# Another stored order of issue for all engines of an attention and channel-mix kernel

## The chip, the cores and the metric

The kernel runs on one core of a Trainium2 chip. Times are device microseconds of that core: the median of several executions, and one execution that the hardware profiler recorded, with its span from the first to the last instruction. The names of the engines in the profile are PE (TensorE, matmuls), PEld (its weight loads), DVE (VectorE), ACT (ScalarE), POOL (GpSimd) and SP (SyncE, which issues the transfers).

## The reference

Attention with queries averaged in pairs, over 8 batches and 8 heads, 1152 keys of 64 elements; then a channel mix over the attention's output, which is regarded as 8 sequences of 576 rows and 512 columns. All in float32.

```python
q_pool = q.reshape(B, H, S // 2, 2, D).mean(axis=3)            # 8, 8, 576, 64
scores = 1.0 / np.sqrt(D) * np.matmul(q_pool, k.transpose(0, 1, 3, 2))
attn = np.exp(scores - np.max(scores, axis=-1, keepdims=True))
attn = attn / (np.sum(attn, axis=-1, keepdims=True) + 1e-09)
x = np.matmul(attn, v).transpose(0, 2, 1, 3).reshape(8, 576, 512)
x_prev = x shifted by one row, zeros first
xk = mu_k * x + (1.0 - mu_k) * x_prev;  xr = mu_r * x + (1.0 - mu_r) * x_prev
kk = np.maximum(xk @ w_k, 0.0)                                 # 512 to 1024
out = 1.0 / (1.0 + np.exp(-(xr @ w_r))) * (kk * kk @ w_v)      # 1024 to 512
```

## The kernel before

**Numbers.** Operands are split into a high and a low 16-bit part, and products are summed from two or three matmuls on these parts in float32.

**Attention.** There are 64 heads (`n`), and each has 6 blocks (`j`) of 96 pooled queries, 384 blocks in all. A block goes through a chain that visits three engines. TensorE computes 9 score matmuls of 96 columns (L555, in two steps of 4 and 5) into one of three PSUM buffers `s`. VectorE takes the maximum over a block's keys (L562). TensorE transposes it (L565), VectorE reduces it again (L569), and TensorE spreads its negative (L571). ScalarE writes it into a row of the low part of the queries (L575). TensorE adds the second half of the scores with that row (L581, again 4 and 5 matmuls), and ScalarE takes the exponential into `pf` (L587). GpSimd makes its low part (L590). Five windows of queries per head are then multiplied with the values into the one PSUM buffer `a` (L624, L627, L629 and L634), which ScalarE and VectorE empty and normalise (L650 to L686).

**Preparation of heads.** Queries and keys are loaded, split on ScalarE, VectorE and GpSimd (L442, L445, L449, L488, L493), and transposed by a transfer; values are split on ScalarE and VectorE (L522, L525). For the very first head TensorE transposes instead, and ScalarE and VectorE copy the results out of PSUM: the keys for the first scores (L501, L502) and for the second (L513, L514).

**Channel mix.** Once a batch's 8 heads are done, tiles of 256 rows are mixed with their previous rows (L800, L803, L809, L811) and go through three products: 18 tiles with 96 matmuls of 256 columns and 2 x 36 of 512 columns (L831), with ScalarE, VectorE and GpSimd steps on their results (L858 to L895). A batch's mix runs beside the next batches' attention. The weights are loaded and split in the first microseconds.

**The order.** All steps are first collected in a list `ops` with their buffers read and written, from which the dependences follow. Then `Issue.run` reads, for each of the five queues (transfers, VectorE, ScalarE, TensorE, GpSimd), the order of its steps from the stored string `TURNS`: each byte says which of the steps that are left, counted in program order, is issued next.

```python
turns = iter(zlib.decompress(base64.b85decode(turns)))
for e in ENGINES:
    left = [n for n in range(len(ops)) if eng[n] == e]
    while left:
        k = 0
        while (step := next(turns)) == 255:
            k += 255
        order.append(left.pop(k + step))
```

Each engine keeps to that order. A step that waits for another engine therefore holds everything behind it in its own list. `Issue.gaps` puts spare matmuls on zeros (L937) into pauses of TensorE that the planned order has in the first 150 us.

Of the kernel before, what the change touches and what calls it, by code (L numbers as in the profile page):

```python
# [37 lines left out]
LO, VLO = 2.0 ** -28, 2.0 ** -12  # L38
# [17 lines left out]
    ")8(Mc@#X9S3bP4&!b>uFHJz?ZE666xlIdg;CCKD*`CKlY)iRlECYFxHVmU3Ft<SQc`umbZG#<(2Q(2~nmPmz@;Z!&rjz^<uEtN^7QyLOMD;A5#tf*"
    "yKv2;A0N~J7$S%SqZvO+2=sL^Q5AB~hm)UXoqhP{^83tuc5gB5Xy!w3cZmKC%l%v`P-R9DwHtE>E#E|=3;=B%!CR-n8Q4Q9PrS5aG8Q&ZVkU6ILTY"
    "Eg|uWql@*s;$$jYpM~8Y0-jKUDI3^kH@uglpzwTt_ejdE5o63;=43cf;<YrP>|bz-=B$Cfq>=LbTyk)(}@HSb4K0ep0L}Qi^UO*X8jJNOot;Ji#wv"
    "G$(~ydrz3(eN5OD9Vu+fR&afFWgQdZaxNZbYBNWo(!GuST8%D&?bv{ENkPiejk5AW<?4ugcRjqMiqt&1_sC9L9nqH%7npRt<*3_siY8|JpzFw`b18"
    "O+F>55csc}*r$mCGq8)YOitNu{c)Qt6D6LRqO2jn?N1P)bXoghH^&Ei0V0j6hD$L=40*&J$BLm&?Ttt1(L(9_5p}yhKW*x;hexLJ#xFX9NlQu(vxD"  # L60
    "O6o+Z88N~}FKKG&R-p9+az+ojgO=45t96)>3nEc7?9hWjL$}X_JeE%W8P$e<stXl<zdzuI&nrpliutDmn*2^f_tcK5Rco~6foi?d(96pUdKpwjD=1"
    "2-qU0;{s3_M^h$rItd>)C!gz=fu81k!lMk$XL;?YvI1^JRlG*XCUk|~6ZAW{L&Tp*g!BYuu?JchARwP^QLbp~1kku#iLH3%hO80W$p3eO4kg+k`aV"
    "9;bA{JxN>TYTtoy6(|ACG6-m0iR#?$J1z8y6H5$#zh=7gYebc0#RDDkRC*%7KoBz;gF{B#3Cz3PSd1l)*Op89J$FH**UUP51H+zVW`90YGYGt+lp3"
    "Ab?cg{HmF$CQqkPp(p*ugl-KK+RjZd5s!&&7x3;di`TTO0SCkY`Q(ID9QsT&?tPG{dX3C9hx=b&@>_nnm>nTH7x+I^ET|jDTskEBRBbQJSPAx?+k<"
    "%?JozA4KRM1Mq;ud%0IORA{>9n3orN^h`@u<utnaoB0vUDkUQYYIz0VI?8q=ysdRg<oGJS(ka%9$Y836`)UOmM|4lNQbsv?e0ZV48KNzN)5nWKB(t"
    "S#7dhuU=GBUFI<Br9mpyD=RB?b|_h!ETocEU6qxn%WK?2tg1pSYb{Tdl||JBkp<CQG+G)dRV55UkuXX~(`*o#bXS@)lgJtIY&J6@6pZA}GeWvFRGA"
    "E`BztrDh%XfN@wo%~RImT0w9n^FcoRfX93HPH;YqY2z9p7PSzeDCPsY78LC#3n?V<gSXzY=LU2-}|Wn;ckZjhx`fChh-9@K-DE6{2h>xQ2{Z1^x;Z"
    "#Er<QCHVe*V0_8yFKiAGu1?Is6V-(9$Kwl)05M3*$U2_T3y|k&8oS&+PX}QmdsRUGWudQSz3h!2~Eis%A&CtB9U-9S`sc%bI4|cvM<SGE>H38NC&O"
    "9lH{5ByiVcD&C7-|p-|qRh#MKJERagVoAqj5k0<5v(B8%{G97ih-HEt%aUkmTBy~06h*ig8YgNuzDC9D!W?`xsA?(l%sS<$#J9%<Ic2oBTlOa83#f"
    "Dpv7Q<*VOj_4seLeYcR+CwMhS^YGVYKM;YvgP~lNPzMO0AUWDl4lht*TVB<H~DO=^C{PN~NNptWXw@#`B1l71+Uio~yEOIDZ1B=5pbz-IWmX31s6L"  # L70
    "y(6ucSXMqK=QHE;bKrf5W}_*eH|g_fh$K?(q}#0~WG_7)kLnIO3GqmnLTtq_CK`>pso@B@EN39n5^=bkx)s#}rXyrpx?WNmkW|*)Ze2GVWH>v{3^G"
    "@vyCaiE4+U-yADhV@8#rB1VZiRK#uF-~lg@?VR27593Yaiv{FpJ5mC=(Xp*Ue|u{gSjF&I5<v^u(2oK#dgMuOz;RFvZMsiTWiitVG6w$6@@*7gzYt"
    "!-_s7!I_x4{IIQ*4o-)3`2`Dbr_nOo7#pc!^hPRYpHK(ZZ@0h(9obX)KdU!s%z?N>g(#->uQafDpWO9S5=`Bqbka4&|Zz2ipr|W$}+XQQZFknDOG4"
    "U3kpheC0QB=oR&i>lOczasXR`elj+stz1oSf6K5$i5t%_d8kruQK64soO%3;ir=5T))22+F7@HECKu2LhSQ$5AlpkZqc6OpT)(QZgqPt_%$WiPd(B"
    "f)#sKb=H=3#Y;(PTCnRrN-rUf-mmv7t~8rK$#H)n%21((;lD-Jmw1)YNh%sl3Cmhm?LN!j)mNv@8}=bI~A4pNK}Ra7<MqO4vu>`hq@1@zVJWhy89J"
    "3SL(LnHIlaf!AAWn(i<?(Q?b>aVoBP1{^xAJ^@a<ZUzlws-c^T^!&PDj-O>Z#wuf#(WARZYsFEc$0)_3g5szV7}Y+iUC!32UF{vCFrpJ3%E;mEozv"
    "(-wY0S~w+=U3TG&0Kv7-@6Ydsnim9B7k6>*^$d6YZL+-5ePZAfS9(isCV5{jWkTa-w%62{6<Fj*6>j>PHLL?R1-kUvE4#zJ6J5S3PiHxLX3$VyMZ-"
    "{A3i;Pt?b5oJM-*Xed=d<q&p9>wD}4CiT%0_Z%K$=;F8OPsTu^r0y()?6bzg*~O03`fsceGJ__4U;=M%#INl(ca!6dpUi?{1M$9ZD?)NThTgf7$>i"
    "}xpSC~=7~zvaJ8{zOpDr7r`Fc1suz<d*Mcx>EJt~v0&qA>r?^NBN8U6!Woi0GNdj1nDZ@EUG}8z!3tLM<OG435d3$tmgpNfZKwDNHEJgxWND2C9TE"
    "P%nf-OGFXDNPv4F}M}nd2I6ug~veM?F=hNoUvt$6A-`eBJp&kM5BUAW3MN>(-fu?6}MHEm)}Q^XFd(%$qwG+R1SAs`GKu>>r?a&YXVZq*=4(%z<&@"  # L80
    "i9MK!l|3^~IHBjH$c!2KtP`e9)2HimF;zpiI%P7H3($pei@ff!=pF+UyU1|USlrp!KHW51TU$GfHU%xihRsq5RZMGWXlbZ#s<(zUz(Q?9^$FE=b+q"
    "vmypvEp9yJXWJ=GOewN*8=Bd&^4Pf1yMnX1sSq&J3iZdf6wrwnsFJ#1a4E1gJgNh*lvE=;P)L^!S>6pIDRY0DxjBf(%OG@HQ}Z5oj>eQFphx=-r%`"
    "KFvXdGcg}u4}?-cNZqOUE?OWCyX6Go<(Ekj~O|#cnU_Lv(wN!_0EpA5k|*?&JJUQ&W^P<w>GOSEiJ0j)Q$G$`sOC9advav%wS_<ZDVbHJ!&yA)J3C"
    "GQwuuIHU63!R8<wK3KbRODhdtd%8VIRK6hb6c|k2#)v~Ngzd4noRmqsCRwG$fnoTFtDFu2`Q7htV?1FeG6p36MVYebyBpi-K)>TBU^NEU3AUL1m3V"
    "$l@w`QLaB(eQ7faz}cw5ijkPQ|))(*8KR-QLN-<cTJF(KY+biCyM|31h~LqsKAYDC)+9*~N}=#Zet26&-3vYwHNDt*s3huHv*4TAGG851Tu87?g%4"
    "rD+^HThCyj0rjXut+%R~HfeOVw+f6Ks=ZTCSyoo=Eui3(^8`m4lk?eJwz*_{%49rbW=CcdiF8{sm2t#VDIkiNmVgpt$P=YVH-%P*8diliT9KedMXL"
    "<bOr1@F(?PP}^ZSzsoE{DI1Uw$!bOomby1TK|>6|<X=#qFFw~F(3vOZ3qF!oGSA3J8zm{Frg>BUhBjcbRd%xZ5Np%&ZQ(b1-y(yp{Y8Q#<+d5b2cv"
    "Av#xQQxR2v&J+wHPklL)|0(N>IAo^q8jC>C@Xgtob8Oo3rePmvCf!Ml+f_%nM9ghOl9&3qdv<XWunO_EgCz-hYya5un(b7l<^yh9cn_5j+Z|WgjGN"
    "V9R@E$dyhBg^(q7{12Vu=eDIpODMeOB+*C_OnMN!r<rHx)R1Nsy_RBC^#-P;DNL)sv!6<D<2s8#X=N`Ap0G#I(J6Z+Q<6C>5noF}HV{10&_XApKsp"
    "fW5!_$oP{S<42HO(pSWq28o@HkJglJnqV>;uyTpA|kM5bzp?+YLtDmNSuXI(<=JE*J6nIDbr;Xqszc!9tez17lOUhR1?k!OO4`bhJY5WYTT9`6%Hu"  # L90
    "QlXNPq04Csk&os080?wX%V0s4SuC~WL(Al(Bkl}1oqQ-(N~c}Kk<)fPbOcIDcmY+<$K#j}@wivENVDi;5eLA-o4MVAcpw%Cq|*qOAe4*S&6buX>?a"
    "7@_u*sN17-n9B<$v7j}y*7j6H_zQ_`Q1-C-+oH0<Z}B$JSH<dG&l9CmT=oN##QM9@sT1Ia)lpGagm{xlgrpMBr*und&h1-qLZU^?7khVzo-Y(5gP@"
    "4$P@apousuka2HmGB841m{VFm^E4SuYbw)cSEHnvn>4*`1ac`zW7@Bh5u`zLMUH-C7k$99uE$FGdL&<2EP;fcY}ivyjB>W{_E54J{2xze9Eg23kRF"
    "~`fJ%V(^ns|b@k{`fuln+A|%jw>yNQ--$$Q(v=4s<K6(Rt_kMg}@B4%J^mTlISMlC^z@bCHo+C&0?D;$J0-k^S`H%3&eZX^gbMIa}`^K|x?S1?0H{"
    "X2r-FMmG8y|l7^wW3?*#8QTUV38B6HfrY!HbXMu|ML`=U#mDQI`Mj8v}cvdyZ`}?cwswE3Z8G;DdPTf!{x{>wyRGyPrS#G@g0petG)tyYI$hczoBc"
    "NAJY1@d$o}Up~s>C!W~3bLTI1;=h1faPz}A<0jn5;(NK=dg~qAw{O2~`}XfyboniK06zzA*vW&7?*KO6fUCKC%Qj%cWtVN+fbISL*Ysa4%P!%vdGp"
    "qx3oq*1y7lU-`!-?Kg{!b~<w~IciY=F8J+SnG3opQuCD^ofE$gk{v}y6;AFjP*?P8hEU%VJtv<|D+uSef`3sx;yux1Tb%l1|P+*`M9*)m}E?Aa_ib"
    "LLF+oOX848Z2BmV+OCA4mwNAm!CdwUN@CsGUebD-sj}5u2V4wC)rO`EcW#FoLnsS7H3iUP91p)FPg^kDO@H_pEGAz*RTmw=v}vTwM>}O(t;CC;E9H"
    "Dm@%WC7ju6seb@?&ESIUPtGu<Nl{+XDS_&B1-igN6M!HF$y&b{pTGPdJI^But##B{GCNx$;REUcDii$*{I#HDnnS>}6r3nbyzNjc?j)@pVf;?xyBT"
    "^#EEcZwq3112Qu#jvJapnL#vW7=;#3L+^Od<@oNHV)17`E7~@UXs%SKG|_{BwEwb2|yQTodL;$Px(0*I$44osDjxGLsyKNd@6JeE6Hgb`p;7z984W"  # L100
    "`TX-k$BrGc)0eW^Az>apbVz8jE#M2ABZ^QyJMhJU1IM9s=<lQe$%PL-IK1!BP}yt1EBGsS-hTVQ+wV&_lSqHS`>($a{OwP`|8To&|0{ocWf$;!{O;"
    "ez{Z9i-uMG@5KR{UjJN;*uh<%uV-ua8Wciz8KBK<BF-gW%st#{sc=e^r^4uSl?Bu#E1&~Lu+MqCD53jFZ4Yj7)Y<(2sH=FK;39=hm9xc>U9F1@tBp"
    "BVlTaK(>t4Q@RDN7v)Lt>^vFuCWbUuI%gUyS#4`*Vx?OkBhKzBWXfX$nzHfMEKc@H!a?{c=0*dLOlOqAxI9M>pS&SoV%VF$FgOs&go@3t9M!NxyyU"
    "cCSP#&*-Mt3c;boNL(iI?9-M~7%L)30tWK<VcQ5T;!rfC>te7-u5hhNYGf^Ucd{56D;6ws{-e{aUdvWo!VsU1%hrkDYg*nqZdOPM!o!ZmUfe|Cnjc"
    "!Q+8}74bH#LoIveUSxCZ3dO1SXHJnOLOHRLv`j7+*QAvUAFm%E}QVDmyDHY1PX|4d*hdh2A3TlS3m%wjd`{u`Y+sY_=*}Sx4^yO&B79<Uk@($wj0k"
# [872 lines left out]
```

## Time and profile before

| what | value |
|---|---|
| median of 3 executions | 1097.0 us (1094.77 to 1098.14) |
| profiled execution, its own time | 1095.32 us |
| its span | 1093.5 us |
| granted clock of TensorE, mean | 1.00 |
| busy: PE, DVE, ACT, POOL | 1071.0, 886.8, 867.7, 808.6 us |
| moved by transfers | 134.77 MB |

The span is what the rows are measured in; the profiled execution's own time is 1.8 us longer than it. Busy times are sums of drawn durations: matmuls are drawn longer than they keep the engine, since they overlap.

### The profile page before, as it was taken

The numbers are of one execution on the slowest core, as the hardware profiler recorded it, in microseconds if no ns is written. First come the engines' busy times: TensorE is split into PE (matmuls) and PEld (weight loads), VectorE is DVE, ScalarE is ACT, GpSimd is POOL, SyncE is SP. The second block draws the span as 40 slices with busy tenths as digits, with TensorE's granted clock in tenths as the row PEclk, the third lists the DMA queues.
The fourth block names the chain that finished last, engine by engine and source line by source line (L and its number), as shares of the span: only waits on it lengthen the run. The fifth ranks groups of instructions, "written<-read, shape, count | busy, mean of one in ns | idle before, by whom it ended". The sixth has DMA issues, their size and how long they took to land. (4 is left out here: it accounts for less than half of the span.)

```text
span 1093.5 us, 40142 instructions
## 1 busy us (share of the span) xinstructions
PE 1071.0 (98%) x16475; PEld 880.5 (81%) x16475; DVE 886.8 (81%) x1869; ACT 867.7 (79%) x1918; POOL 808.6 (74%) x940
## 2 busy tenths in 40 slices
...
GB/s 215 200 237 203 187 124 147 139 125 147 127 117 154 123 115 143 129 133 123 101 115 126 127 121 116 129 115 142 104 140 134 94 142 84 96 49 34 10 30 31
DMA packets 257387, 134.77 MB, mean 123 GB/s; under 512 B 192753, under 2 KB 229617, under 8 KB 257201
## 3 DMA queue, kind: packets, MB, share of 16 engines
...
q8 instruction: 129, 2.11, 0.8%
...
## 5 line engine op out<-in xcount | busy, mean ns | idle before, releaser
L562 DVE TENSOR_REDUCE mx<-s 128x96 f16<-128x864 f32 x384 | 400.4, 1053 | 69.4 <-PE s L555 40.1
L590 POOL TENSOR_SCALAR pl<-pf 128x864 f16<-128x864 uint16 (+1 forms) x384 | 334.1, 870 | 109.3 <-ACT pf L587 65.8
L587 ACT ACTIVATE pf<-s 128x864 int32<-128x864 f32 x384 | 336.5, 888 | 62.2 <-PE s L581 45.5
L555 PE MATMUL s<-qT,ks 128*128 128x96 f16 x3456 | 237.4, 206 | 2.9 <-ACT pf L587 1.4
L624 PE MATMUL a<-vt,pf 128*128 128x129 f16 x2520 | 234.9, 220 | 0.9 <-DVE den L667 0.6
L581 PE MATMUL s<-qT,ks 128*128 128x96 f16 x3456 | 230.3, 206 | 0.9 <-ACT qT L575 0.4
L555 PEld LDWEIGHTS <-ks 128*128 128x128 f16 x3456 | 191.3, 98 | 25.4 <-issue 3.5
L581 PEld LDWEIGHTS <-ks 128*128 128x128 f16 x3456 | 188.8, 98 | 25.1 <-issue 1.8
L624 PEld LDWEIGHTS <-pf 128*128 128x128 f16 x2520 | 169.0, 98 | 23.5 <-issue 1.6
L569 DVE TENSOR_REDUCE mb<-s 128x1 f16<-128x128 f32 x384 | 108.7, 287 | 42.7 <-PE s L565 37.0
L575 ACT ACTIVATE qT<-s 1x96 f16<-1x96 f32 x384 | 90.1, 236 | 67.0 <-PE s L571 56.9
L634 PE MATMUL a<-vb,pl 128*128 128x65 f16 x2304 | 136.1, 193 | 0.0
L831 PE MATMUL f<-xhk,wk_lo 128*128 128x256 f16 x496 | 135.2, 273 | 0.0
L831 PE MATMUL f<-xhk,wk_hi 128*128 128x256 f16 x496 | 135.2, 273 | 0.0
L831 PE MATMUL f<-xlk,wk_hi 128*128 128x256 f16 x496 | 135.2, 273 | 0.0
L634 PEld LDWEIGHTS <-pl 128*128 128x128 f16 x2304 | 111.1, 98 | 15.4
L831 PEld LDWEIGHTS <-wk_hi 128*128 128x128 f16 x1152 | 104.0, 98 | 13.3
L493 POOL TENSOR_TENSOR kn<-kr,kn 128x320 f16<-128x320 f32 (+1 forms) x126 | 98.9, 789 | 15.5 <-ACT kn L488 9.3
L862 POOL TENSOR_TENSOR gl<-g 128x512 f16<-128x512 f32 x72 | 76.6, 1068 | 43.9 <-ACT g L860 40.6
L831 PE MATMUL f<-wv_hi,g 128*128 128x512 f16 x240 | 90.9, 379 | 0.7 <-ACT ex L879 0.7
L831 PE MATMUL f<-wv_hi,gl 128*128 128x512 f16 x240 | 91.0, 379 | 0.0
L831 PE MATMUL f<-wv_lo,g 128*128 128x512 f16 x240 | 90.9, 379 | 0.0
(128 smaller groups left out, 2166.1 us busy)
## 6 DMA issues: line engine op xcount, KB each, us to landing
...
```

The costliest lines, as they stand in the source:

```text
L493: lambda cs=cs, en=nc.vector if ve else nc.gpsimd: en.tensor_tensor(kn[i][:, cs, D:P], kr[i][:, cs], kn[i][:, cs, 0:D], op=ALU.subtract),
L555: nc.tensor.matmul(cols(c, c + 1), ks1[hp][:, c, :], qhi, start=(c == c0), stop=False, skip_group_check=True)
L562: op("DVE", 0.974, lambda: nc.vector.tensor_reduce(mxz[:, P - QN:P], grid(0, NC).rearrange("p c q -> p q c"), axis=AX.X, op=ALU.max), r=[( ...
L569: op("DVE", 0.199, lambda: nc.vector.tensor_reduce(mbz, s[:, 0:P], axis=AX.X, op=ALU.max), r=[("s", z)], w=[("mb", z)], key=t + O_MAX)
L575: op("ACT", 0.15, lambda: nc.scalar.activation(qlo[0:1], s[0:1, 0:QN], AF.Prelu, scale=1.0 - EPS, alpha=(1.0 + EPS) / (1.0 - EPS)), r=[("s ...
L581: nc.tensor.matmul(cols(c, c + 1), ks2[hp][:, c, :], qlo, start=False, stop=True, skip_group_check=True)
L587: op("ACT", NC * QN / 1200 + 0.051, lambda: nc.scalar.activation(pf[:, :, HALF + rows.start:HALF + rows.stop], grid(0, NC), AF.Exp, bias=S ...
L590: op("POOL", 0.93 if buf == ("pside",) else NC * (r1 - r0) / 1200 + 0.273, lambda: nc.gpsimd.tensor_scalar(to, half(pf, U16, 0)[:, :, HALF ...
L624: nc.tensor.matmul(a_b[:, a0:a0 + D + VN], half(pf, F16, 1)[:, c, his], vt[jv][:, c, 0:D + VN], start=(first and c == 0), stop=(side and c ...
L634: nc.tensor.matmul(av, pl[:, c, rows], vb[jv][:, c, 0:VN], start=False, stop=(c == NC - 1), skip_group_check=True)
L831: nc.tensor.matmul(ps, terms[i][0], terms[i][1], start=(first and i == 0), stop=(i == last), skip_group_check=True)
L862: op("POOL", 2 * n * 0.0018 + 0.14, lambda f2=f2: nc.gpsimd.tensor_tensor(gl[:, f2, 0:n], g32[:, f2, 0:n], gh[:, f2, 0:n], op=ALU.subtract ...
```

## The change

The string `TURNS` is replaced, and nothing else. Both strings hold the same number of steps for each queue, and the steps, their operands and their buffers are the same; the dependences still hold. The core of the diff, 100 lines of encoded text in place of 101:

```diff
 TURNS = (
-    "c-mch37i$hx&7(&?)UcH_j_mN&b|-K3^Q<9hh+d65XOa7R6v#iS6~n#XfP@+L2=E)7<Y~OOyWdMG!dU-qT+MI1eYYJXbggmL=m^t|5Ohq@At3z^;T"
...
+    "c-m!pcYqbu{r#Ex=JlCZ=Jm4W?Y@26cU@Svuq-S^dRYO*0wO4~Dp*kw6-#1AG>K8rBo^$(NP<aBf=Y}=qTj?4j7Ag1M58En4eI>PoyGXa@7|raGjq"
...
 )
```

Decoded, the two lists compare as follows. A neighbour pair is two steps that directly follow each other in both lists.

| queue | steps | at the same place | neighbour pairs kept | mean shift, places | largest shift |
|---|---|---|---|---|---|
| transfers | 496 | 120 | 89 | 2.1 | 16 |
| DVE | 1851 | 301 | 401 | 4.1 | 58 |
| ACT | 1917 | 249 | 387 | 4.5 | 47 |
| PE | 5948 | 1071 | 1475 | 3.0 | 30 |
| POOL | 932 | 121 | 104 | 3.7 | 33 |

The heads of two lists, as an example (`c0` and `c5` are the first five and the last four of the nine key chunks):

```
ACT before: L445 qn, L488 kn c0, L488 kn c5, L467 qT, L488 head 1 c5, L513 keys for the second product, L501 keys for the first, L488 head 1 c0, L404, L467, L522 c5, L522 c0, L445, L575 block 2, ...
ACT after:  L445 qn, L488 kn c5, L488 kn c0, L467 qT, L404, L488 head 1 c0, L501 keys for the first, L488 head 1 c5, L513 keys for the second product, L467, L445, L522 c0, L522 head 1 c0, L522 c5, L488 head 2 c0, L575 block 2, ...
DVE before: L442, L493 c0, L493 c5, L449, L514, L502, L442, L562 block 2, L562 block 0, L569 block 2, ...
DVE after:  L442, L493 c5, L493 c0, L449, L502, L442, L514, L562 block 0, L562 block 2, L449, L569 block 2, ...
```

## Rows read from the trace of the kernel before

**Rows 1.** The page: span, and busy time, share and instructions of engines.

```profile
span 1093.5 us, 40142 instructions
...
PE 1071.0 (98%) x16475; PEld 880.5 (81%) x16475; DVE 886.8 (81%) x1869; ACT 867.7 (79%) x1918; POOL 808.6 (74%) x940
```

**Rows 2.** Windows: length, busy PE, PEld, DVE, ACT, POOL, then PEclk, DMA share, GB/s.

```profile
0.00:60.00 60.00, 51.51 (x1086) 46.72 (x1087) 49.31 (x110) 48.25 (x101) 38.79 (x53) 1.00 0.96 215
60.00:130.00 70.00, 66.69 (x1428) 60.87 (x1425) 67.00 (x130) 67.41 (x149) 61.43 (x70) 1.00 0.78 198
130.00:200.00 70.00, 67.69 (x1014) 55.11 (x1012) 63.59 (x121) 61.04 (x135) 57.39 (x64) 1.00 0.60 146
200.00:600.00 400.00, 397.58 (x6186) 329.98 (x6185) 347.80 (x744) 328.71 (x738) 314.59 (x367) 1.00 0.59 128
600.00:1000.00 400.00, 398.34 (x6194) 332.83 (x6193) 333.62 (x717) 317.45 (x709) 304.76 (x351) 1.00 0.50 110
```

**Rows 3.** Timeline of PE: start, drawn us, line, tile, shape, count, idle before it.

```profile
0.99 3.62 PE L937 MATMUL a<-zero 128*128 128x128 f16 x33 [0.99 <-DVE kn L372]
...
304.42 0.44 PE L634 MATMUL a<-vb,pl 128*128 128x65 f16 x9
304.69 0.33 PE L624 MATMUL a<-vt,pf 128*128 128x129 f16 x3
304.86 0.38 PE L555 MATMUL s<-qT,ks 128*128 128x96 f16 x5
...
306.87 0.55 PE L581 MATMUL s<-qT,ks 128*128 128x96 f16 x9
307.25 0.27 PE L831 MATMUL f<-xhk,wk_hi 128*128 128x256 f16 x1
...
308.33 0.27 PE L831 MATMUL f<-xhk,wk_hi 128*128 128x256 f16 x1
...
309.20 0.33 PE L581 MATMUL s<-qT,ks 128*128 128x96 f16 x4
...
1089.13 0.38 PE L831 MATMUL s<-wv_hi,g 128*128 128x512 f16 x1
...
1089.56 0.38 PE L831 MATMUL s<-wv_hi,gl 128*128 128x512 f16 x1
```

**Rows 4.** DVE groups by line: whole run, whole run, to 130 us, from 130.

```profile
L562 DVE TENSOR_REDUCE mx<-s 128x96 f16<-128x864 f32 x384 | 400.4, 1053 | 69.4 <-PE s L555 40.1
...
L569 DVE TENSOR_REDUCE mb<-s 128x1 f16<-128x128 f32 x384 | 108.7, 287 | 42.7 <-PE s L565 37.0
...
L525 DVE SCALAR_TENSOR_TENSOR vt<-vr,vt 128x256 f16<-128x256 f32 (+1 forms) x18 | 8.5, 481 | 0.0
...
L525 DVE SCALAR_TENSOR_TENSOR vt<-vr,vt 128x320 f16<-128x320 f32 (+1 forms) x110 | 66.0, 603 | 0.3 <-ACT vt L522 0.2
```

**Rows 5.** Timeline of DVE, POOL and PE around 343 us.

```profile
340.94 0.32 DVE L803 SCALAR_TENSOR_TENSOR xk<-xt,mu_k,tmp 128x128 f32<-128x128 f32 x1
...
342.60 1.65 POOL L696 TENSOR_TENSOR st<-xb,st 128x640 f16<-128x640 f32 x1 [2.29 <-ACT st L694]
...
342.91 1.49 DVE L803 SCALAR_TENSOR_TENSOR xk<-xt,mu_k,tmp 128x128 f32<-128x128 f32 x1
...
344.32 1.04 DVE L562 TENSOR_REDUCE mx<-s 128x96 f16<-128x864 f32 x1
...
345.43 0.23 PE L565 MATMUL s<-identb,mx 128*128 128x128 f16 x1 [1.39 <-DVE mx L562]
```

**Rows 6.** Timeline of ACT and PE at the start of the run.

```profile
7.24 0.69 ACT L513 COPY ks<-s 64x640 f16<-64x640 f16 x1 [0.37 <-DVE ks L514]
...
7.95 0.69 ACT L501 COPY ks<-s 128x640 f16<-128x640 f16 x1
...
8.70 0.94 PE L555 MATMUL s<-qT,ks 128*128 128x96 f16 x18 [0.90 <-ACT ks L501]
...
12.22 0.44 ACT L575 ACTIVATE qT<-s 1x96 f16<-1x96 f32 x2 [1.36 <-PE s L937]
```

More of the change, by code (lines that the diff above doesn't have):

```diff
@@ L56 @@
[L56 to L105, printed above, removed]
@@ new lines @@
+    "$*m`!Msmo?&C%&~@AGC?km}Fbr=vW*Aw+U}GchgE#L9W<7@K(KstU&PLG#Pgu>UP!vP+XvMH6s%eU<1bm2bnu9sRFlCSI_r^?kINQ3IY}NE~>>dxN"
+    "U4_oO;2^nFB1zCCus382az2A}38`GFI+aOD$sF?ed?BCD<dkeSm$fstZReF7Q{~$e$yg#*C>EH~N-Ua8C$gz%IvS0}qcJ7LZqg|wnUHNWZpY1-X`1"
+    "nL#!jV7wgO_YcqkeQSs@eQxHyVc#e&fQtW?w=G5vmjkY{awI1-KctPsLsGaU9ZHK6Qms4p9JbwR_ZF^qDZQ7WMY&3cpGSgO=DG_;n=+1hNj(tuQb8"
+    "p%pJ)ley`^{7*9rA8??B&rgLTGZHx)HPHh<yb5dtt~{VBUM%rr2=ZKh=oEplrznc6*gsAN$2ELDh(vcKASfdHByO0HsQ@1exH$+Ql3<jQyq`!Q8O~"
+    "eV|Zd7Pb89RiRd0Z9tS*8)#|ZSQw`_10#UIOwl%dJgA!3tZJA0q98iL)B6Emwu2}2jNtUO%xrHNA8)a24D@tRNQjr_fHsVBXZjzfCfre}*n<+Jx(h"
@@ new lines @@
+    "a$6eLfG=jBjj^%4JA(oaS^oUX?5sYPrPmVtph^G?yY)G-Xzqri!c*gdLwaL9zV-zsebwRj!d7gV(UoXjg1Ifw-3w!yBGyavTv=oot#uJFE}H^uwY&"
+    "t-1>`ljdcqR`ZZ)dgE$L6MgmQmPM?c5IQ6p3r1AG7S@>90HIJggg_u5&roD<C>#qJL~P@P#>W2Dl}d$|Dc9FQQe{ahDz%bS&HqxNR9Avjn@lE)#p0"
+    "A=It{66psGqnUBR|%YEUiJ2+M3nt(MCo60ve&ZH{H8!i8Ko9Ewj-(`pj%`C^0=K^Y34ABuH`<a4pq(oBzzV6;9K^{Cbehhb_#J*ZhzEQ{b#bvhH%G"
+    "RIk5u&V@+0-}mf(;9*oL}OfHP6}s%z9`5!5Yrk{l}JQUXy{9;O`DEQQzDjP(o6NuIj_&^>Fw<?qF!T+N?#?Ptc)4kCLiKyQWdeRP}@swZS8HPQb|H"
+    "%qf#l=qN%2-v2lvhHiWgcrP}7EW?F4SS+B$LY__JR;b`Qlh{SA7CR5aquT@YZ%f)yh9w$n()$t6Zd=gnHQx%OAt@c75xg760y)a@XbE-Wro2kyIF)"
@@ new lines @@
+    "m{^JUJ91Sko!`bvqO4&V*9ur3whC0fm-?)G4V{B9sV+(iz2{3?u?suir-xX~g3OqR|+wD<QnA79mNr3O}P)D*cTkm7a>#KtR+rHhI+QvR2>BTEZ0S"
+    "=GLW4rMelV>7@#7wLV>kQe(c7Nvn|SODmP-c1^8ZU93vT2|E@mRuyA)1w>-eh-AUcW~bz`YKF5MPUI4~$f}H$?kZ|3-Bl!`n(1_!MWOk2CL5+5B=e"
+    "@34TM6OU|<5x+O~TG@jw8HWWtZQFC9v89CpGh$73;tj(0@(Dh?{;HGGK2%bufn$Cjm8W_SUuI6&WE&47nPY(Jx;v!lIT*Ui-)U2SY{Y;QYGZB+wxE"
+    "Nj)(=4SpiHO)hzqR^9~(ntWe=JQ3lQLZ$uLZu;Jkfi0MY(=hVuoHF3Ogd4Gq#cjf#Anx3qq=IEEfwr&EL)8XiUrH!+Et-w6|AGRTrTe}rJ4_gv}{c"
+    "_6GS*<hBBc*Agv^l1BrgvS>dWu$)qnBXv<_bWaPA*^2r|C6X((;Igf~wY?w69QeE>4r)QZ((>#o38zhV)W7RRXu21PyJ3AuL_BOg+O>1w|R%$KUGV"
@@ new lines @@
+    "*Vwy~34Ln-?_!3n~>kTjovCAIX(Wx!jVM3ys-yrkp8*Yg<Z6NE}s_Ow^W86R(yMc8UHzRt;i$S}`7vOEt)(i|K-u*H9gfSj7Sds^)T*#kDjO`7DAV"
+    "HKhatariU-v@a7+#*>MJ?1${Lyk;V9#5_K)mGE-S`ZzGJ&l|Bc!w5xbekN%(?1|9w!eK4M;brL$(mLrk6wp=Er^2B7^^v_jvPg=mLG$@XDN+!q>Xj"
+    "k8yBZW#oEHS@ktH%Z1fTL~=3qYt`uc|Yh9>nb;7)&^G#>qOUr%3e?@+JQJr3RDy1QpeQtzQ%y*)icJ>6a1-E#NXL&l6b1c!7=W5z07W4gLJ`XROUw"
+    "6;NRZ)qc`b)c=Szp=Hqt+lnK1(l|z=B5f78Y-2hURu|oXzZ$#8_H$5Twh-=Rq84r0icXhU2CaC*I1J3Yl~Gi#UiS40<EVCg~HN8Udm;%QZ|!;wlJx"
+    "#7)EM1J<pyu7jqDsMZnFRf84B@vH0BSvDvX%z>KL=549&voitaHhag4!CPjM3Pngh)@vs78fxe)xx5wAx>uw+0?r#&SqD|@;*DAHQO>Lt~S6kX;ik"
```

129 lines of the change are left out of this document (79 added, 50 removed).

## The prediction

> **What bounds the kernel now.** I read the totals first: TensorE is busy 1071.0 of 1093.5 us, every other engine 74 to 81% [rows 1]. A drawn matmul lasts longer than it occupies the engine, so small gaps hide in that 98%. I therefore took the steps from one start to the next where nothing waits [rows 3]: nine matmuls of 96 columns take 307.25 - 306.87 = 0.38 us (42 ns each), three of 129 columns 304.86 - 304.69 = 0.17 (57 ns), nine of 65 columns 304.69 - 304.42 = 0.27 (30 ns), eight of 256 columns 309.20 - 308.33 = 0.87 (109 ns), two of 512 columns 1089.56 - 1089.13 = 0.43 (215 ns). The code issues 6912, 2520, 3024, 1728 and 1296 of these, 384 more of 128 and 384 of 96 columns for the row maxima, 48 transpositions (4 us), and the trace has 179 spare ones on zeros (55 ns each). That is 292 + 143 + 91 + 188 + 279 + 37 + 4 + 10, a floor of about 1043 us. One microsecond passes before the first matmul and 3.7 after the last one's step (1089.56 + 0.22 to 1093.5) [rows 1, 3]. So TensorE waits about 1093.5 - 1043 - 4.7 = 46 us, and no order can win more than that.
>
> Where do these 46 us lie? The windows [rows 2] show 8.5 us of visible idle before 60 us, 3.3 up to 130, 2.3 up to 200, and then 4.1 in the 800 us up to 1000. Adding the hidden gaps, from every matmul's start against these steps (the first and the last start stand in [rows 3], 16475 matmuls), some 33 us lie before 200 us and about 9 between 200 and 1000, counting gaps over 0.1 us. Before 130 us there is hardly any channel-mix work for TensorE. There VectorE and ScalarE are the limit, at 67.0 and 67.4 of 70 us, and TensorE waits for them. Later TensorE is the bound, and only stray stalls cost time.
>
> One such stall can be followed [rows 5]. The step of L803 on 128 columns takes 0.32 us at 340.94, but 1.49 at 342.91. GpSimd's L696 had started at 342.60 and ended at 344.25, and L803 ended 0.15 us after that. The maximum L562 behind it on VectorE started only at 344.32, and TensorE's L565 got its operand at 345.43, after 1.39 us of idle. What ended late here was one step that came out longer than its neighbours of the same shape.
>
> **The change part by part.** No instruction is added or taken away, apart from spare matmuls, whose number follows from the order (179 x 55 ns is 10 us in all, placed in early pauses). At their own durations the lists of each engine sum to the same work. What changes is who stands in front of whom. Decoded, both lists run side by side: the work that stands ahead of a given block's maximum on VectorE, exponential on ScalarE or scores on TensorE differs by under 2 us at most of the 50 blocks that I compared, with either sign. The work before the first channel-mix matmul on TensorE is 81 us in both. So the large-scale plan is the same, and I cost local differences.
>
> *Start.* Before, ScalarE copies the keys for the second product (L513, 7.24 us) ahead of those for the first (L501, 7.95), and the first scores start at 8.70 [rows 6]. The new list has L501 first, so these scores can start one copy, 0.7 us, earlier. But it also puts the key conversion L488 of a later head and a value conversion L522, about 0.9 us of work, ahead of the first L575 at 12.22. ScalarE had idled 1.36 us there [rows 6], so the block comes at the same time and 0.9 us of work is done early. ScalarE and VectorE are 96% busy from 60 to 130 us, so this can shorten the stage by 0 to 0.9 us; I take 0.6, since nearly all of that stage is work.
>
> *Slack inside a block.* After a block's scores TensorE needs the maximum (1.05 us, [rows 4]) before L565, then the second reduction (0.29) before L571, then L575 (0.22, [rows 6]) before L581. With 0.3 us for the two hand-overs (an estimate: 0.07 of it is from the maximum's end at 345.36 to L565 at 345.43 [rows 5], the rest the way in) these links need 1.4, 0.6 and 0.55 us of other TensorE work between. I summed the steps between them in either list, for the 324 blocks after the 60th. Short of that plus 0.3 us are 61, 98 and 195 links before, and 46, 106 and 177 after; what they lack together falls from 67 to 58 us, by 14%. With 1.0 us instead of 0.3, about one such lengthening, it falls from 467 to 456 us, by 2%. Taken as shares of the 9 us of late stalls this is worth 0.2 to 1.3 us; I take 0.5, nearer the lower end, because the stall followed above was of the long kind.
>
> *Steps that meet on VectorE and GpSimd.* L525 takes 481 ns on average before 130 us, where 18 stand, and 603 ns after, where 110 stand [rows 4]. The same step is thus 122 ns dearer in the crowded stage, and L803 shows single ones 1.2 us dearer. Any new order deals these meetings anew. I take no change, with 3 us either way: some 28 steps at 122 ns, or two or three stalls like that at 345.43. The Trainium skill, "SBUF — State Buffer", section "Who interferes with whom", says that a VectorE step with two operands in SBUF and a GpSimd step that reads SBUF hold one port pair in turn, the later one waiting for the whole of the earlier. This trace agrees at 342.91. By that rule a meeting could cost the whole of GpSimd's 1.65 us; by the rows its average is 0.12 us, and my sum uses the latter.
>
> *Transfers.* They move by 2.1 places on average, 16 at most. The transfer engines are 0.96 busy up to 60 us and 0.5 to 0.6 after 200 [rows 2]; the early loads are what a bad place could hurt. The first four stand unchanged, and I cost the rest at nothing, covered by work on the buffers of the head before. A wrong one would cost a late head at ScalarE, priced with the slower rival.
>
> *End.* The last 48 matmul steps alternate between the same two products and end with the same four; VectorE's last step and the store follow in both. Nothing changes.
>
> Sum: -0.6 - 0.5 = -1.1 us, on a profiled execution of 1095.3 (its span and 1.8 us around it). The median of the runs is 1.7 us above it, so I forecast 1097.0 - 1.1, rounded to 1096 us; as bounds, -0.9 - 1.3 - 3 = -5.2 and +3 - 0.2 = +2.8 give 1091.8 to 1099.8 for this case.
>
> **Rivals.** *Faster:* the new order has room exactly where steps lengthen. Half of the 9 us of late stalls goes, and 0.9 at the start: 1097.0 - 5.4 = 1091.6. For it speaks that the sum lacking at 0.3 us falls by 14%; against it, that at 1.0 us it hardly falls. It decides once over a quarter of the late stalls goes with the start's gain. *Slower:* meetings of VectorE and GpSimd enter the first 130 us. There VectorE has nothing to spare, and 18 steps of L525 [rows 4] and, by the code, 24 like it for the queries of the first heads (L442, L449, also with two operands in SBUF) stand in its list. At 122 ns more each that is 42 x 0.122 = 5.1 us, and all later work moves with it: 1102.1, or 1101.0 after the gains. Against it: in the list of before only few of them meet, and the new one has the same steps in almost the same places. It decides from 4.4 us, some 36 of the 42 steps, or four whole waits of 1.1 us. A load that comes late there does the same with one wait of 4 to 5 us. *No effect at all:* the lists differ everywhere, but differences may cancel; that is 1097.0, inside the forecast's own range.
>
> **How the numbers follow.** A difference under 0.3%, 3.3 us, can hardly be told from none here: the runs before span 1094.8 to 1098.1. Forecast case, same: 0.55. Its neighbour faster than 1093.7: 0.28, since the slack counts lean that way and the stalls offer up to 9 us. Slower than 1100.3: 0.17, of which late loads hold 0.04. The range 1090.5 to 1101 takes in the bounds of the forecast and the centre of the faster rival, and most of the slower one; it leaves out about 0.1 on either side.
>
> **What would show it.** Right: the first scores start near 8.0 us; VectorE's and ScalarE's busy time from 60 to 130 us stays near 67; L525 stays near 480 ns there; TensorE's visible idle from 200 to 1000 us is between 2.5 and 5 us; the granted clock stays 1.00 as in every window before [rows 2]. The forecast is wrong if the late idle falls under 2 us (the faster rival), or if TensorE's idle before 200 us grows by over 3 us, with L525 near 600 ns there (the slower one) or with ScalarE waiting for a load.

## The result, and the profile after

The changed kernel takes 1101.56 us (median of 6 executions, 1101.01 to 1104.46) against 1097.25 for the kernel before in the same session: a ratio of 1.0051, 95% interval 1.0034 to 1.0069. It is 4.3 us slower. The forecast was 1096 us, and its range ended at 1101.0, so the time lies 0.6 us outside.

The executions that were profiled lie 9 us apart, more than the medians: the changed kernel's is the slowest of its six (1104.46 us, span 1102.6), and that of before is near its fastest (1095.32, span 1093.5). A second profile of either order, taken in the experiments, has spans of 1103.2 and 1095.8.

The page of the changed kernel, to be held against [rows 1]:

```profile
span 1102.6 us, 40082 instructions
...
PE 1073.3 (97%) x16469; PEld 880.5 (80%) x16469; DVE 897.9 (81%) x1869; ACT 870.5 (79%) x1918; POOL 807.6 (73%) x940
```

VectorE's busy time grew most, by 11.1 us on the same 1869 instructions (by 6.9 us between the second profiles, from 890.7 to 897.6). TensorE has six fewer matmuls, since the new order leaves room for 173 spare ones instead of 179.

The windows of the changed kernel, in the columns of [rows 2]:

```profile
0.00:60.00 60.00, 51.17 (x1052) 45.97 (x1053) 48.95 (x109) 47.96 (x100) 37.02 (x51) 1.00 0.96 210
60.00:130.00 70.00, 64.31 (x1402) 58.32 (x1402) 65.78 (x124) 65.29 (x142) 59.52 (x69) 1.00 0.82 196
130.00:200.00 70.00, 65.57 (x976) 53.17 (x975) 63.75 (x120) 59.57 (x131) 56.77 (x63) 1.00 0.58 146
200.00:600.00 400.00, 396.45 (x6159) 328.72 (x6156) 351.25 (x736) 326.56 (x733) 313.22 (x363) 1.00 0.60 126
600.00:1000.00 400.00, 397.21 (x6190) 332.69 (x6187) 336.12 (x719) 319.19 (x709) 303.46 (x353) 1.00 0.54 113
```

No single stage holds the loss, but two thirds of it lie before 200 us. TensorE's visible idle grows from 8.5 to 8.8 us before 60 us, from 3.3 to 5.7 up to 130, from 2.3 to 4.4 up to 200, and from 4.1 to 6.3 in the 800 us after. From 60 to 130 us VectorE and ScalarE, which were to stay near 67 us, are also less busy (65.78 and 65.29): they wait, too.

**One account for all kernels.** For each matmul I took the time to the next one's start, less the median of such times for the same operation and shape; summed, this is what TensorE pauses, drawn overlap left out. In the kernel before the pauses sum to 47.4 us, and span less pauses is 1046.1; in the changed kernel 56.5 and 1046.1. So the work is the same, and the whole difference of the two spans is pauses: 3.3 us more of them before 130 us and 5.7 more after. Between the second profiles of the two orders it is 5.4 us before 130 us and 2.0 after. So how the loss divides at 130 us depends on the executions compared, and the four pairings put 37 to 73% of it before 130 us.

**What the late pauses are.** After 130 us the kernel before has 8 pauses of 0.45 us or more, 6.5 us together; the changed kernel has 16, 11.8 us together. That difference of 5.3 us is nearly all of the 5.7 (in the second profiles 11 with 9.1 us and 17 with 12.6). Ahead of every one of them stands, in the 2.6 us before, a VectorE step that came out over 0.25 us longer than the undisturbed ones of its kind (the fifth percentile of before), always one with two operands in SBUF beside a GpSimd step. Such a step stands ahead of only about a third of all matmuls after 130 us. One of the largest pauses, in the timeline of the changed kernel:

```profile
926.36 1.40 POOL L695 TENSOR_TENSOR st<-xb,st 128x640 f16<-128x640 f32 x1
...
926.37 1.53 DVE L802 SCALAR_TENSOR_TENSOR xr<-xt,mu_r,tmp 128x128 f32<-128x128 f32 x1
927.83 0.48 DVE L568 TENSOR_REDUCE mb<-s 128x1 f16<-128x128 f32 x2
...
928.16 0.22 PE L570 MATMUL s<-negi,mb 128*128 128x96 f16 x1 [0.87 <-DVE mb L568]
```

GpSimd's subtraction started 0.01 us ahead of the mix step, which then ended 0.14 us after it and took 1.53 us instead of 0.34. The reduction behind it on VectorE, with no part in this, started 1.2 us late, and TensorE stood still for it. It is the picture of [rows 5] at another place. The Trainium skill, "SBUF — State Buffer", section "Who interferes with whom", lists a VectorE step with two inputs in SBUF as contending with a GpSimd step that reads SBUF, and calls the port pair that they share an exclusive lock. This row agrees, with 1.40 us of GpSimd inside 1.53 of VectorE.

Two things limit this reading. First, the new order does not lengthen many more steps: after 130 us 133 and 139 VectorE steps are lengthened in that way in the two profiles of before, and 145 and 144 in those of the new order. What differs is how many of them make TensorE pause. Second, a lengthened step ahead of a pause need not be its cause. The last of these pauses in each order, 0.90 us at 1008 us in before and 0.46 us at 1017 us in the changed kernel, is ended by a ScalarE step, and comes back at the same matmul and in the same size in the experiment without two-operand steps. Its row in before, and then in `nolock_before`:

```profile
1008.29 0.38 PE L831 MATMUL f<-wv_hi,g 128*128 128x512 f16 x1 [0.74 <-ACT ex L879]
```

```profile
998.12 0.38 PE L837 MATMUL f<-wv_hi,g 128*128 128x512 f16 x1 [0.73 <-ACT ex L885]
```

The other pauses of 0.45 us or more, 7 in before and 15 in the changed kernel, are gone there or down to half and less.

**The first scores and L525.** Three more rows for [rows 6] and [rows 4]: TensorE's first scores (L554, before L555) in the first and in the second profile of the new order, and the low value part (L524, before L525) to 130 us in the first.

```profile
8.40 0.56 PE L554 MATMUL s<-qT,ks 128*128 128x96 f16 x9 [0.46 <-ACT ks L500]
```

```profile
9.09 0.93 PE L554 MATMUL s<-qT,ks 128*128 128x96 f16 x9
```

```profile
L524 DVE SCALAR_TENSOR_TENSOR vt<-vr,vt 128x320 f16<-128x320 f32 (+1 forms) x18 | 10.2, 568 | 0.0
```

The scores start 0.3 us earlier here, but at 9.09 us in the second profile, against 8.97 in the second of before: that they start earlier is not shown. At 22 us TensorE is 1.0 us behind at equal work (0.7 to 1.7 us over the four pairings of profiles). The 18 low parts take 568 ns on average instead of 481, and 589 instead of 482 in the second profiles. All VectorE steps before 130 us together take 6.4 us beyond their undisturbed durations in both profiles of the new order, against 4.5 and 5.2 in before. So the early pauses grew by more than these steps did.

### The profile page after: what moved, and what is told of

Its sections match the earlier page's. It is cut to its first block, busy times and chain, and to the rows that moved or that the text cites. A ratio compares the mean times of both kernels' runs of the same rounds, so it can differ in the third digit from the quotient of the medians.

```text
span 1102.6 us, 40082 instructions
## 1 busy us (share of the span) xinstructions
PE 1073.3 (97%) x16469; PEld 880.5 (80%) x16469; DVE 897.9 (81%) x1869; ACT 870.5 (79%) x1918; POOL 807.6 (73%) x940
## 5 line engine op out<-in xcount | busy, mean ns | idle before, releaser
L554 PE MATMUL s<-qT,ks 128*128 128x96 f16 x3456 | 239.0, 206 | 2.9 <-ACT pf L586 1.3
L554 PEld LDWEIGHTS <-ks 128*128 128x128 f16 x3456 | 193.8, 98 | 30.2 <-issue 3.6
L633 PEld LDWEIGHTS <-pl 128*128 128x128 f16 x2304 | 109.9, 98 | 16.9 <-issue 1.5
L830 PEld LDWEIGHTS <-wk_hi 128*128 128x128 f16 x1152 | 104.3, 98 | 11.1 <-issue 0.6
L492 POOL TENSOR_TENSOR kn<-kr,kn 128x320 f16<-128x320 f32 (+1 forms) x126 | 97.0, 774 | 19.9 <-ACT kn L487 13.8
```

The source lines that it names most:

```text
L492: lambda cs=cs, en=nc.vector if ve else nc.gpsimd: en.tensor_tensor(kn[i][:, cs, D:P], kr[i][:, cs], kn[i][:, cs, 0:D], op=ALU.subtract),
L554: nc.tensor.matmul(cols(c, c + 1), ks1[hp][:, c, :], qhi, start=(c == c0), stop=False, skip_group_check=True)
L633: nc.tensor.matmul(av, pl[:, c, rows], vb[jv][:, c, 0:VN], start=False, stop=(c == NC - 1), skip_group_check=True)
L830: nc.tensor.matmul(ps, terms[i][0], terms[i][1], start=(first and i == 0), stop=(i == last), skip_group_check=True)
```

## The experiments

Eleven kernels ran. Each is compared with the kernel before in its own session. The columns "pauses" are worked out from the profiled execution as above: before 130 us, after it, and the number and sum of those of 0.45 us or more after 130 us. In every kernel span less all pauses is 1045.9 to 1047.4.

| kernel | median us | ratio, 95% interval | its span | pauses to 130 | after 130 | 0.45 us or more |
|---|---|---|---|---|---|---|
| before | 1097.25 | 1 | 1093.5 | 28.3 | 19.2 | 8, 6.5 |
| before_again | 1097.54 (one execution) | | 1095.8 | 27.3 | 22.4 | 11, 9.1 |
| after | 1101.56 | 1.0051 [1.0034, 1.0069] | 1102.6 | 31.6 | 24.9 | 16, 11.8 |
| after_again | 1101.56 | 1.0046 [1.0028, 1.0064] | 1103.2 | 32.7 | 24.4 | 17, 12.6 |
| a130_b | 1100.93 | 1.0034 [1.0020, 1.0047] | 1096.9 | 29.7 | 19.9 | 9, 7.2 |
| b130_a | 1100.66 | 1.0037 [1.0023, 1.0050] | 1098.4 | 27.9 | 23.7 | 15, 10.5 |
| b600_a | 1101.77 | 1.0039 [1.0026, 1.0051] | 1099.7 | 27.1 | 26.5 | 14, 12.3 |
| a_thin | 1103.66 | 1.0054 [1.0042, 1.0067] | 1099.4 | 28.7 | 24.8 | 15, 11.2 |
| nolock_before | 1086.04 | 0.9895 [0.9881, 0.9908] | 1083.6 | 27.0 | 9.9 | 2, 1.4 |
| nolock_after | 1086.75 | 0.9897 [0.9882, 0.9912] | 1085.5 | 29.2 | 10.2 | 3, 1.5 |
| a_late | 1101.73 | 1.0049 [1.0034, 1.0064] | 1101.5 | 30.6 | 24.3 | 14, 10.5 |
| a_swap | 1097.66 | 1.0008 [0.9998, 1.0018] | 1097.0 | 29.8 | 21.2 | 12, 8.0 |
| b_swap | 1093.56 | 0.9969 [0.9958, 0.9979] | 1091.8 | 28.6 | 16.9 | 7, 4.7 |

A profiled execution need not be a typical one (that of a130_b is 2 us under its median, that of after 3 us over), so verdicts on times go by the medians, and the columns on the right say where pauses lie. The theory that I brought to them: the loss is meetings of VectorE and GpSimd. The rivals: the new order's own waits, and a late load or instruction fetch.

### Both orders again

The two kernels as they are, for second profiles.

> The changed kernel once more, for a second trace and a tighter ratio. Both theories expect 1099 to 1103 us, a ratio to the kernel before of 1.004 to 1.006. If the pauses of TensorE without a releaser (1.3 to 1.6 us idle at 25.6, 39.0 and 112.1 us of the first trace) belong to the order, all three come back at the same matmuls; if they are luck of one execution, the third is gone and the time is 1 to 2 us nearer to that before.

> The kernel before once more, for a second trace of it. Time 1094 to 1098 us. If the meetings of VectorE and GpSimd steps belong to the order, the mean of L525 before 130 us is again 475 to 490 ns, and TensorE's longest pause after 200 us is again the one before L565 near 345 us; if they are luck, both change.

The result stands: 1101.56 us again. Of the three pauses without a releaser only the one at 112 us comes back in full (1.93 us of idle); the other two shrink from 1.4 and 1.7 us of pause to 0.7 and 0.4. The mean of L525 to 130 us is 482 ns again in before, as expected of a property of the order. The second profile of before is of use, because it shows which pauses belong to the order. The stall of [rows 5] comes back in it to the hundredth, 1.55 us of pause beside the same two steps, and so do the seven other pauses of 0.45 us or more. Three come new, among them this one, where the first profile has nothing (timeline of the second profile of before):

```profile
247.60 1.41 POOL L696 TENSOR_TENSOR st<-xb,st 128x640 f16<-128x640 f32 x1 [0.22 <-ACT st L694]
...
247.85 1.37 DVE L803 SCALAR_TENSOR_TENSOR xk<-xt,mu_k,tmp 128x192 f32<-128x192 f32 x1
249.15 1.04 DVE L562 TENSOR_REDUCE mx<-s 128x96 f16<-128x864 f32 x1
...
250.45 0.22 PE L571 MATMUL s<-negi,mb 128*128 128x96 f16 x1 [0.76 <-DVE mb L569]
```

So a meeting is mostly a property of the order, and in part of how far the engines have come when they get there. The three new ones are 2.7 us, and the two spans of this one kernel lie 2.3 us apart.

### Half of the new order

`a130_b` has the new order for the steps that the plan of before starts in its first 130 us, and the old one for the rest; `b130_a` is the reverse. `b600_a` has the old order up to 600 us and the new one behind.

```python
early = {n for n in steps if start_in_plan_of_before[n] < 130}
order[e] = [n for n in new[e] if n in early] + [n for n in old[e] if n not in early]
```

> The new order for the steps that the plan of before starts in its first 130 us, the old order for all others. Theory early (the new order loses its time in the DVE- and ACT-bound start): 3 to 6 us slower than before. Theory spread (many small stalls, everywhere): within 1 us of before.

> The reverse: the old order for the steps that the plan of before starts in its first 130 us, the new order for all others. Theory early: within 2 us of before. Theory spread: 3 to 5 us slower than before, like the whole new order.

> The order of before for all steps that its plan starts in the first 600 us, the new order for the rest. The new order after 130 us alone cost 0.37 % (4.0 us). If that loss lies in the channel mix's second part, where TensorE's pauses were 1.5 to 2 us longer in each run with the new order there (7.0, 6.4, 7.2 against 5.5, 5.4, 5.1), this kernel is 1.5 to 2.5 us over before, ratio 1.0014 to 1.0023. If it lies in 130 to 600 us, it is within 0.7 us of before (0.9994 to 1.0006). A full 4 us (1.0037) would say that all of it lies after 600 us.

Each half costs nearly as much as the whole: 0.34, 0.37 and 0.39%. So `a130_b` came out as the early theory had it and `b130_a` as the spread one had it, and neither theory holds. The parts don't add up, and these times can't place the loss. `b600_a` came out at the last of the cases named for it, the full loss, although its order up to 600 us is the old one. At equal work its profile stays within 0.4 us of before's second one up to 570 us. Then comes the largest late pause in any of the profiles, where the two lists join, at a place at which neither parent pauses (timeline):

```profile
576.77 0.98 POOL L585 TENSOR_SCALAR pl<-pf 128x864 f16<-128x864 uint16 x1
...
576.91 1.18 DVE L444 SCALAR_TENSOR_TENSOR qn<-qs,qn 128x320 f16<-128x320 f32 x1
578.02 0.28 DVE L564 TENSOR_REDUCE mb<-s 128x1 f16<-128x128 f32 x1
...
578.35 0.22 PE L566 MATMUL s<-negi,mb 128*128 128x96 f16 x1 [1.75 <-DVE mb L564]
```

Behind that it has the new order's meeting of 926 us as well (1.03 us). Joining two lists deals meetings of its own.

### A load burst and TensorE's instruction fetch

In both profiles of the new order TensorE stops inside one step at the same matmul, the 2138th, with nothing to wait for; in none of before. These two profiled executions are the slowest of their sets (1104.46 and 1105.04 us); whether the other executions stop there, too, is not known. First the row, then the windows of the changed kernel around it, in the columns of [rows 2]:

```profile
112.13 0.34 PE L633 MATMUL a<-vb,pl 128*128 128x65 f16 x6 [1.41 <-issue]
```

```profile
104.00:109.50 5.50, 5.25 (x132) 4.83 (x130) 5.24 (x12) 5.39 (x11) 5.01 (x7) 1.00 0.98 256
109.50:110.60 1.10, 1.10 (x35) 1.10 (x32) 1.10 (x3) 1.10 (x5) 1.10 (x1) 1.00 0.06 15
110.60:112.00 1.40, 0.12 (x4) 0.03 (x1) 1.00 (x2) 1.40 (x4) 1.31 (x3) 1.00 0.00 0
```

The queue of instruction packets (129 packets of 16 KB in the run) shows TensorE's next block, fetched at 103.8 us in before (at matmul 2014), only at 109.6 here (at matmul 2113), after five transfers issued from 101.3 to 105.2 us had filled the engines (share 0.98). `a_thin` moves two of these, the q and the v rows, ten microseconds back in the transfer list:

```diff
-... w_v, vr, qTl, kr, qr, w_v, ks1, kr, vr, ks2, ...
+... w_v, qTl, kr, w_v, ks1, kr, vr, ks2, qr, vr, ...
```

> The changed kernel with two loads moved back in the transfer list, by some 10 us: the q rows and the v rows that stand in the burst between 101 and 105 us, and whose data no step takes before 122 us. All other steps keep their places. Theory (TensorE's instruction fetch waits behind the burst): the fetch that started at 109.2 to 109.6 us starts before 107, the pause of TensorE at matmul 2138 (1.6 and 2.1 us) is gone, and the time falls by 1.5 to 2.5 us, to a ratio of 1.0022 to 1.0035 to before. Rival (the pause comes from the matmuls' own place, not from the loads): pause and time stay, ratio 1.0046.

The fetch came earlier (105.0 us, at matmul 2060), and the pause at matmul 2138 is gone, so its cause is shown. The median did not fall: 1103.66 us. In the profiled execution the gain was kept: the pauses are 28.7 us before 130 us, against 31.6 and 32.7, and 24.8 after as they were, and its span is 3.2 and 3.8 us shorter. But that execution is the fastest of its five, and the two that it is held against are the slowest of theirs. By the medians the fetch is not the cause of the loss; why removing the pause wins nothing in them is open.

### Both orders without two-operand steps on VectorE

Six groups of VectorE steps become reductions over an added axis of size 1, which read one operand from SBUF. What they leave out is in the expectation. Two of the six:

```diff
-nc.vector.tensor_tensor(qs[0][:, js], qr[0][:, js, 0:D], qr[0][:, js, D:2 * D], op=ALU.add)
+nc.vector.tensor_reduce(qs[0][:, js], qr[0][:, js, 0:D].unsqueeze(3), axis=AX.X, op=ALU.max)
-nc.vector.scalar_tensor_tensor(xm[w][:, c, o0:o0 + ln], x[:, c, s0 + 1:s0 + 1 + ln], m[:, c:c + 1], tmp[z][:, 0:ln],
-    op0=ALU.mult, op1=ALU.add)
+nc.vector.tensor_reduce(xm[w][:, c, o0:o0 + ln], tmp[z][:, 0:ln].unsqueeze(2), axis=AX.X, op=ALU.max)
```

> The order of before, but six groups of VectorE steps no longer read two operands from on-chip memory (L442 query pairs, L449 and L525 low parts, L672 division, L803 mix, L886 gate): each becomes a reduction over an added axis of size 1 with as many elements out, and so a copy. Left out are: odd query rows, the true low parts of queries and values, the division by the denominators, the previous-row part of the mix, and the tanh factor of the gate; V is scaled by 2^-22 so that sums stay finite. GpSimd keeps its steps. Theory (meetings of VectorE and GpSimd): steps keep one duration each, GpSimd's shorten too, and the excess of VectorE's steps over their undisturbed durations falls from 95 us over the run to under 25. TensorE's pauses from 200 to 600 us stay as they were in the quieter run of before (7.5 us) or fall. Time 1088 to 1097 us. Rival (the waits are the order's own, meetings are hidden): excess falls too, but pauses and time stay, 1095 to 1099.

> The same edit on the changed kernel's order, so that the two orders stand against each other with no two-operand steps on VectorE. Theory (the loss is meetings that the new order makes more frequent): the distance between the two falls from 4.5 us to under 2; TensorE's pauses from 200 to 600 us, 10 against 7.5 with meetings, are within 1 us of each other. Rival (the new order's own places for steps and transfers): the distance stays 3.5 to 5.5 us, with the pauses before 130 us still 3 us longer.

This experiment weighs most. Between the same two orders 0.7 us are left of 4.3 (1086.75 against 1086.04), and the ratios to before have nearly the same interval. Both are faster than the 1088 to 1097 us that I expected. The groups by line, first of `nolock_before`, then of `nolock_after` (low value part, mix for the gate, and, in the first, GpSimd's low part of the exponentials):

```profile
L532 DVE TENSOR_REDUCE vt<-vt 128x256 uint16<-128x256 uint8 (+1 forms) x128 | 56.0, 441 | 0.7 <-ACT vt L529 0.5
L810 DVE TENSOR_REDUCE xr<-tmp 128x256 f32<-128x256 f32 (+3 forms) x96 | 32.4, 343 | 36.9 <-ACT tmp L807 18.8 <-PE f L837 12.1 <-ACT ex L885 3.8
...
L597 POOL TENSOR_SCALAR pl<-pf 128x864 f16<-128x864 uint16 (+1 forms) x384 | 320.3, 834 | 121.9 <-ACT pf L594 75.7 <-ACT qT L582 6.5 <-PE s L572 5.6
```

```profile
L531 DVE TENSOR_REDUCE vt<-vt 128x256 uint16<-128x256 uint8 (+1 forms) x128 | 56.1, 442 | 0.6 <-ACT vt L528 0.5
L809 DVE TENSOR_REDUCE xr<-tmp 128x256 f32<-128x256 f32 (+3 forms) x96 | 32.5, 344 | 22.2 <-PE s L836 9.1 <-PE f L836 7.0 <-ACT tmp L806 5.8
```

These steps have one duration each, whatever the order: 441 and 442 ns for the low value part, which took about 600 [rows 4], while GpSimd works beside them; its own L597 takes 834 and 833 ns on average in the two, against 870 in before. What VectorE's steps take beyond their undisturbed durations falls from 99 us (before) and 108 (after) to 16 in both, TensorE's pauses after 130 us from 19 and 25 to 10 in both, and no pause of 0.45 us behind a lengthened VectorE step is left. Before 130 us the new order still pauses 2.2 us longer in these profiles, so a part of the early loss is its own. One rival stays beside the meetings: the reductions are also shorter than undisturbed two-operand steps, 232 against 249 us for all 596. So of the 96 us that these steps lose (334 to 237 us in the old order) 17 are less work, and a VectorE with more room could hide differences of order by itself. The moves in the next section leave every step's work as it is. In the windows from 200 to 600 us TensorE's visible idle is 0.43 us of 400 in `nolock_before` (first row) and 0.52 in `nolock_after`, where before has 2.42 [rows 2]:

```profile
200.00:600.00 400.00, 399.57 (x6232) 332.02 (x6230) 312.69 (x750) 330.63 (x743) 301.52 (x367) 1.00 0.59 129
```

```profile
200.00:600.00 400.00, 399.48 (x6230) 332.33 (x6227) 311.96 (x749) 329.62 (x741) 299.35 (x365) 1.00 0.62 128
```

That such a reduction never meets GpSimd is what the Trainium skill says of it on trn2, on the page and in the section named above; these rows agree.

### Single meetings taken out of either order

If single meetings cost time, moving the VectorE steps that had them must win time in either order, with every other list left as it is. `a_late` moves three steps of the new order by one place, `a_swap` twelve by one or two, `b_swap` six of the old order, each behind the step that it held up, or ahead of a maximum where VectorE or GpSimd was idle. VectorE's list around three of the places, by lines of before:

```diff
 a_late, a_swap at 926 us
-... L672, L672, L562, L803, L569 ...
+... L672, L672, L803, L562, L569 ...
 b_swap at 343 us
-... L886, L803, L562, L569 ...
+... L886, L562, L803, L569 ...
 b_swap and a_swap at 248 us
-... L803, L562, L569, L886 ...
+... L562, L569, L803, L886 ...
```

> The changed kernel with three VectorE steps moved by one place each near its end, all else as it was: the low query part (L448) that ran beside GpSimd's subtraction of L695 goes behind the maximum that waited for it (pause of TensorE of 0.64 us at 897 us), the mix step (L802) at 926.4 us goes ahead of the maximum before it, into VectorE's idle time (1.03 us at 928), and the low value part (L524) at 941.4 us does so too (0.56 us at 943). Theory (the loss is single meetings that stand in the order and come in every run): nothing before 890 us changes, the three pauses go, and the time falls by 1.5 to 2.2 us, to a ratio of 1.002 to 1.0032 to before. Rival (such a pause only takes up slack that is lost anyway, as with the instruction fetch, whose pause went without gain): the ratio stays at 1.0042 to 1.005.

> The changed kernel with twelve VectorE steps moved by one or two places, wherever after 150 us a step with two operands from on-chip memory ran beside a long GpSimd step and TensorE then waited for the maximum queued behind it; GpSimd, ScalarE, TensorE and the transfers keep their order. The pauses at these places add up to 9.0 us in the profiled run. What moves earlier shifts the meetings behind it, so that not all is kept. Theory: the time falls by 3 to 6 us, to 1095.5 to 1098.5, ratio 0.998 to 1.001; TensorE's pauses after 130 us fall from 24 us to 16 to 20. Rival (as many new meetings arise as are taken away): within 1 us of the changed kernel, ratio 1.0036 to 1.0054.

> The kernel before with six VectorE steps moved by one or two places behind the maximum that waited for them (places at 142, 184, 248, 343, 535 and 608 us in its traces, with pauses of TensorE of 1.01, 0.73, 0.92, 1.55, 0.58 and 0.54 us; the one at 248 is in one of its two traces). All else keeps its order. Theory (single meetings set the difference of any two such orders): 1.5 to 3.5 us faster than before, ratio 0.9968 to 0.9986. Rival (new meetings arise for those taken away): no change, 0.9993 to 1.0007, or slower.

`a_swap` wins 3.9 us: 1097.66 us, level with before, as expected; its pauses after 130 us, 21.2 us, stay above the 16 to 20 expected. `b_swap` is faster than both kernels, 1093.56 us, by 0.31% (0.21 to 0.42) against before. So single meetings cost time in either order. These two runs alone do not show that meetings make the difference between the orders, since the same treatment wins as much in the old one: with both treated, the distance is still 4.1 us. They fit it, for `a_swap` keeps 12 large pauses with 8.0 us and `b_swap` 7 with 4.7. One of the six moves did not pay: near 186 us `b_swap` pauses 0.94 us, where before paused 0.73. The place of [rows 5] now reads (timeline of `b_swap`):

```profile
342.45 1.66 POOL L692 TENSOR_TENSOR st<-xb,st 128x640 f16<-128x640 f32 x1 [2.28 <-ACT st L690]
...
342.76 1.05 DVE L558 TENSOR_REDUCE mx<-s 128x96 f16<-128x864 f32 x1
343.73 0.52 DVE L799 SCALAR_TENSOR_TENSOR xk<-xt,mu_k,tmp 128x128 f32<-128x128 f32 x1
...
343.87 0.23 PE L561 MATMUL s<-identb,mx 128*128 128x128 f16 x1
```

GpSimd's long step starts as before. The maximum runs beside it untouched, 1.05 us, the mix step meets only the end of it, and TensorE's transposition of that maximum follows without a pause.

`a_late` did not show in the time: 1101.73 us, within the scatter of the changed kernel. In its profile the three pauses are gone, and TensorE gains 1.8 us on the changed kernel between 890 and 1010 us, of the 2.2 us they summed to. A pause of 0.75 us at 869 us, ahead of the first step moved, which neither profile of the changed kernel has, takes 0.7 of it back. That is less than medians of six runs can tell here, so its expectation on the time failed, and by its time alone it is inconclusive.

## Why the prediction was wrong

**What bounds the kernel: right.** The floor held in all profiles, 1046 us with both ends against 1043 + 4.7, and everything that moved was pauses.

**Same plan on the large scale, nothing at the end: right.** The pauses after 1000 us are 0.8 to 0.9 us in either order.

**Start, -0.6: wrong.** The first scores start 0.3 us earlier in one pair of profiles and 0.1 later in the other, and TensorE is 0.7 to 1.7 us behind at 22 us, and 0.9 us without two-operand steps. The gain at one hand-over said nothing of the next ones. What exactly costs that microsecond was not tried.

**Slack inside a block, -0.5: not seen.** The late pauses grew. The growth does not come from links that are a little short, which I had counted: the pauses under 0.45 us after 130 us sum to 12.7 and 13.3 us in before and to 13.1 and 11.8 in the new order. It comes from the large ones, each behind a single VectorE step of 0.8 to 1.9 us. The last large one of each order, which ScalarE ends, is the exception.

**Steps that meet on VectorE and GpSimd, taken as no change: the step that failed.** The mechanism was the one I had described at 342.91; the term was mis-sized. I took zero because a new order deals meetings anew, and so I treated before as an average order. It had 8 or 11 such pauses in its two profiles (6.5 and 9.1 us), the new one 16 and 17 (11.8 and 12.6): a term of +3 to +6 us where I had 0, and the medians are 4.3 us apart. Without two-operand steps they are 0.7 apart, so by the times some 3.6 us go with such steps. The row average of 122 ns was the wrong unit, too; most lengthened steps cost nothing (some 140 of them after 130 us stand against 8 to 17 large pauses), and a few with a reduction behind them cost TensorE 0.5 to 1.9 us each.

**Transfers at nothing: the gap was real, the price right by the medians.** A load burst held up TensorE's instruction fetch, which I had not thought of, but with the pause gone the median was no lower.

**The slower rival** was the nearest: the new order's meetings, with L524 at 568 ns in the first 130 us as its sign, and 1101.0 to 1102.1 us. I had given times over 1100.3 us a chance of 0.17. Its other sign came, too: TensorE's visible idle before 200 us grew by 4.8 us, where it asked for over 3. But it looked for all of the loss in the first 130 us, at 5.1 us for 42 steps. There VectorE's steps are lengthened by only 1 to 2 us more than in before, while TensorE's pauses grow by 3.3 to 5.4 us, and 2.2 us of growth remain without two-operand steps. So the early part of the loss, a third to three quarters by the profiles, is mostly not explained by this price.

**Open.** The new order, its three mixtures and the one with two loads moved all came out 3.4 to 5.4 thousandths above before. That before's list has few large pauses is measured; why its lengthened steps, nearly as many, so seldom stand ahead of a reduction that TensorE waits for is not. What makes up the early part of the loss is open, too. The kernel's own plan does not tell: `Issue.follow`, which lets VectorE's marked two-operand steps and GpSimd's steps run only in turn, gives 1130.1 us for the list of before and 1128.4 for the new one, and so ranks them the wrong way round.
